# A third score buffer borrowed from the second weights, and identity matmuls between the first tile pairs, in a talking-heads attention and feed-forward kernel

## The chip, the core and the metric

The kernel runs on one core of a Trainium2 chip. The core has five engines that work side by side, each through its own instructions in order: PE (TensorE, matmuls into PSUM), ACT (ScalarE), DVE (VectorE), POOL (GpSimd) and SP (SyncE, which here only issues transfers). ACT and POOL issue transfers too, in line with their other work. Sixteen DMA engines carry the transfers of all queues. The metric is the device time of one execution in microseconds (us), as the median of several runs.

The profile gives each PE matmul its start and a modelled end. It also records the clock that the chip granted to PE: 1.0 is full, 0.5 half. The recorded changes of this clock lie on a grid of 3.41 us.

## The reference

Inputs q, k and v have shape (8, 12, 448, 64): 8 batches, 12 heads, 448 positions, 64 numbers a head. Two 12 x 12 matrices mix heads, w_pre before the softmax and w_post after it.

```python
scores = scale * np.matmul(q, k.transpose(0, 1, 3, 2))
scores = np.einsum('bhij,hg->bgij', scores, w_pre)
attn = softmax(scores)
attn = np.einsum('bhij,hg->bgij', attn, w_post)
x = np.matmul(attn, v)            # to (3584, 768), heads side by side
h = np.maximum(x @ w_in, 0.0)     # w_in (768, 2048)
out = h * h @ w_out               # w_out (2048, 768)
```

(The softmax is written out in the reference; it is named here.)

## The kernel before

**Scores.** For each batch, q and k are loaded, turned on PE (`turn_unit`) and kept as qT and kT. Scores are made a block at a time: a block holds 128 queries of one batch, all 12 heads and 448 keys, as bf16 in a tile S of 128 x 12 x 448. A batch has four blocks (0 to 3). A block is filled by six score pairs (`score_pair`, two heads each): four matmuls of 64 x 64 on 448 columns, one on each quarter of the PE array, and two copies from PSUM to S (L312), one on ACT and one on DVE. S has two buffers, so block 2 takes the buffer of block 0 and block 3 that of block 1.

**Gathers.** Mixing heads needs them on partitions. A tile is 10 queries: `gather` (L329) moves 10 x 12 rows of S to the 120 partitions of a tile G, one DMA a tile. A batch has 45 tiles, the whole kernel 360. G has 12 buffers, and gathers run up to 12 tiles ahead. In the first batch the even tiles' gathers are issued by SP and the odd ones' by ACT; later all by SP. Transfers share eight semaphores, and a gather may have to wait, in its issuing queue, for an earlier one on its semaphore.

**The main loop.** A step `ds` (L461) handles two tiles:

- loads that are due (issued by POOL): k and q of batch 1 come in steps 3 to 8, the eight loads of w2 (the second weights, `load_w2`) in steps 9 to 16, one a step;
- `unmix(ds - 2)`: PE applies w_post to the tiles of two steps before (at_ps, L369), DVE copies the result (at, L374);
- `scores_for(ds)`: some score pairs for later blocks;
- `mix(ds)`: PE applies w_pre to two gathered tiles (m_ps, L338), ACT takes the exponential and its sum (e_sb, L343), DVE the reciprocal (rc, L345), POOL scales and subtracts (d, L347);
- gathers for tiles further on;
- filler: the feed-forward work that is ready (ffn1: h_ps, L234; ffn2: o_ps, L267), spread over the steps by `fill`.

After step 9 the first 16 tiles of batch 0 are done, and step 10 begins with `av_unit` (ot_ps, L185), attention times v for them; the first feed-forward filler comes a step later.

Ahead of the loop stand the turning of batch 0, its blocks 0 and 1, the first ten gathers, and the loads of w1 and v.

**What sets the order.** PE and POOL run in the order in which the program is written (`tc.manual_schedule`). The other engines' order comes from the framework's scheduler. PSUM has eight banks, handed out through one pool (`bank`); whoever takes a bank waits for the engine that last read it.

**How many pairs a step issues** is set in `scores_for`. In batch 0 this line paces them, from the position of the step within a block (`into` of `size`):

```python
want = NPAIR * (blk + 1) + -(-NPAIR * into // size)
```

It gives no pairs in steps 0 and 1 and two in step 2. The scores of batch 0's block 2 are made in steps 2 to 7, those of block 3 from step 8 on.

**The second weights.** w2 is held in four tiles of 128 x 4 x 768 bf16, loaded in halves; its first reader is the ffn2 filler that enters at step 25.

Of the kernel before, what the change touches and what calls it, by code (L numbers as in the profile page):

```python
# [8 lines left out]
BF16 = mybir.dt.bfloat16  # L9
# [5 lines left out]
B, H, S, D = 8, 12, 448, 64  # L15
DMODEL = H * D
DFF = 2048
NPAIR = H // 2
FT = DFF // 128
# [11 lines left out]
PARTS = [[0, 16, 32, NT], [0, 15, 31, NT]]  # L31
LAG = 2
# [10 lines left out]
def kernel(  # L43
# [11 lines left out]
    nc = tc.nc  # L55
    P = nc.NUM_PARTITIONS

    consts = ctx.enter_context(tc.tile_pool(name="consts", bufs=1))
    wts = ctx.enter_context(tc.tile_pool(name="wts", bufs=1))
    stage = ctx.enter_context(tc.tile_pool(name="stage", bufs=1))  # L60
    work = ctx.enter_context(tc.tile_pool(name="work", bufs=1))
# [4 lines left out]
    def bank(name, dtype=F32):  # L66
        return psp.tile([P, 512 if dtype == F32 else 1024], dtype, name=name, tag="ps")
# [11 lines left out]
    ident = consts.tile([P, P], BF16, name="ident")  # L79
# [53 lines left out]
    cgblk = consts.tile([P, NPAIR], F32, name="cgblk")  # L133
    wpost_bf = consts.tile([H, H], BF16, name="wpost_bf")
    w1 = [wts.tile([P, NPAIR, DFF // 4], BF16, name=f"w1_{x}") for x in range(4)]
    w2 = [wts.tile([P, FT // 4, DMODEL], BF16, name=f"w2_{x}") for x in range(4)]

    qTs, kTs, bvecs, xts, h2ts, ats = {}, {}, {}, {}, {}, {}

# [59 lines left out]
    def av_units(b, part):  # L199
        return [(800, lambda cp=cp: av_unit(b, part, cp)) for cp in range(2)]  # L200
# [20 lines left out]

    def load_w2(x):
        n = DFF // 8
        c = x % 2 * 2
        nc.gpsimd.dma_start(out=w2[x // 2][:, c:c + 2, :],
                            in_=moe_w_out[n * x:n * x + n, :].rearrange("(c p) m -> p c m", p=P))

    def ffn1_unit(b, ft, half, c0=0, c1=S):
# [22 lines left out]
    def store_rows(b, mt, osb):  # L251
        t, end = 128 * mt, 128 * mt + ROWS[mt]
        while t < end:
            r, p = divmod(t, PR)
            n = min(end - t, PR - p)
            j = t - 128 * mt
            nc.sync.dma_start(out=out_rows[b, r, p:p + n, :], in_=osb[j:j + n, :])
            t += n

    def ffn2_unit(b, mt, nt, part):  # L260
        if part == 0:
            o_open[(b, mt, nt)] = bank("o_ps")
        ps = o_open[(b, mt, nt)]
        for ft in range(4 * part, 4 * part + 4):
            for n2 in ((nt,) if mt < 3 else (0, 1)):
                dst = ps[:, 0:384] if mt < 3 else ps[64 * n2:64 * n2 + 64, 0:384]
                nc.tensor.matmul(dst, lhsT=h2ts[(b, ft)][:, mt * 128:mt * 128 + ROWS[mt]],  # L267
                                 rhs=w2[ft // 4][:, ft % 4, n2 * 384:(n2 + 1) * 384], start=(ft == 0), stop=(ft == FT - 1))
        if part < 3:
            return  # L270
        if mt < 3:
            if nt == 0:
                osbs[b] = ffnp.tile([P, DMODEL], F32, name="osb", tag="osb", bufs=2)
            nc.vector.tensor_copy(out=osbs[b][:, 384 * nt:384 * nt + 384], in_=ps[:, 0:384])  # L274
            if nt == 1:
                store_rows(b, mt, osbs[b])
        else:
            osb = ffnp.tile([P, 384], F32, name="osb3", tag="osb3", bufs=1)
            nc.vector.tensor_copy(out=osb[:, :], in_=ps[:, 0:384])
            r, p = divmod(128 * mt, PR)  # L280
            for n2 in range(2):
                nc.sync.dma_start(out=out_rows[b, r, p:p + 64, n2 * 384:(n2 + 1) * 384],
                                  in_=osb[64 * n2:64 * n2 + 64, :])
# [13 lines left out]
    Sb, Gs, dsb = {}, {}, {}  # L297

    def score_pair(n):

        b, blk, p = n // (4 * NPAIR), n // NPAIR % 4, n % NPAIR
        if (b, blk) not in Sb:
            Sb[(b, blk)] = work.tile([P, H, S], BF16, name="S", tag="S", bufs=2)
        pss = [bank("s_ps") for _ in range(2)]
        for hh in range(2):
            rs = slice(64 * hh, 64 * hh + 64)
            for z in (0, 64):
                q0 = BLK_START[blk] + z
                nc.tensor.matmul(pss[hh][z:z + 64, 0:S], lhsT=qTs[b][rs, p, q0:q0 + 64], rhs=kTs[b][rs, p, :],  # L309
                                 start=True, stop=True)  # L310
        for hh, copy in enumerate((nc.scalar.copy, nc.vector.tensor_copy)):
            copy(out=Sb[(b, blk)][:, 2 * p + hh, :], in_=pss[hh][:, 0:S])  # L312
# [4 lines left out]
    def needs(s):  # L317
        b, t = s
        return 4 * NPAIR * b + NPAIR * (t // TPB + 1)
# [61 lines left out]
    def at_step(i, unit):  # L381
        timed.setdefault(i, []).append(unit)

    def fill(ns):
# [5 lines left out]
        if not filler:  # L390
            owed[0] = min(owed[0], 0.0)

    steps = [(b, t) for b in range(B) for t in range(NT)]
    with tc.manual_schedule(engines={PE, POOL}):
        for x in range(4):
# [9 lines left out]
        def at_load(i, f, *args):  # L405
            loads.setdefault(i, []).append(lambda: f(*args))
# [6 lines left out]
        for x in range(2, 8):  # L413
            at_load(-1, load_w1, x)
        for x in range(8):
            at_load(18 + 2 * x, load_w2, x)
        for x in range(6):
            at_load(6 + 2 * x, load_qk, 1, x)
            at_load(46 + 2 * x, load_qk, 2, x)
# [12 lines left out]
        def scores_for(ds, most):  # L432
            tile = 2 * ds + AHEAD + 2
            blk = sum(tile >= x for x in starts) - 1
            if blk + 1 >= len(blocks):
                want = NPAIR * len(blocks)
            elif blk in (3, 4):
                want = NPAIR * 4 + 2 * max(0, ds - FIRST_TURN[0])
            else:
                into, size = tile - starts[blk] - 2, starts[blk + 1] - starts[blk] - 2  # L440
                want = NPAIR * (blk + 1) + -(-NPAIR * into // size)
            want = min(want, issued[0] + most, NPAIR * min(blk + 2, len(blocks)))
            k = min(2 * ds + 8, len(steps) - 1)
            want = max(want, needs(steps[k]))
            while issued[0] < want and issued[0] % NPAIR < turned.get(issued[0] // (4 * NPAIR), 0):
                score_pair(issued[0])
                issued[0] += 1

        def gathers_for(ds):
            while gathered[0] < min(2 * ds + AHEAD + 2, len(steps)):  # L450
                if issued[0] < needs(steps[gathered[0]]):
                    break
                gather(gathered[0])
                gathered[0] += 1

        gathers_for(-1)
        for n in range(NPAIR, 2 * NPAIR):
            score_pair(n)
        for f in loads.get(-1, []):
            f()  # L460
        for ds in range(nd + LAG):  # L461
            for i in (2 * ds, 2 * ds + 1):
                for f in loads.get(i, []):
                    f()
            now2 = steps[2 * ds:2 * ds + 2]
            old2 = steps[2 * (ds - LAG):2 * (ds - LAG) + 2] if ds >= LAG else []
            for b, t in now2:
                if t == 0:
                    if b == 0:
                        at_step(ds + 6, (100, cg_unit))  # L470
                    if b + 1 < B:
                        for x, u in enumerate(turn_units(b + 1)):
                            at_step(ds + TURN.get(b, TURN[B])[x], u)
            rest = ((NT + 1) // 2 + LAG + 2 - ds) % (NT / 2) + 1
            if EARLY[2] < ds <= EARLY[2] + 2:
                rest = NT // 2
            elif ds <= EARLY[2]:
                rest = 1 + min(x for x in EARLY if x >= ds) - ds
            share = sum(w for w, _ in filler) / rest if now2 else 1e9
            now = timed.pop(ds, [])  # L480
            for w, f in now:
                f()
            if old2:
                unmix(ds - LAG)
                for b1, t1 in old2:
                    ends = PARTS[b1 % 2]
                    if t1 + 1 in ends:
                        part = ends.index(t1 + 1) - 1
                        for x, u in enumerate(av_units(b1, part)):
                            at_step(ds + (2 + x if b1 else 1), u)  # L490
                        if b1 == 0:
                            c = (IQ * ends[part], min(IQ * ends[part + 1], S))
                            at_step(ds + 1, (0, lambda c=c: filler.extend(ffn1_units(0, *c))))
                    if t1 == NT - 1:
                        if b1 > 0:
                            at_step(ds + 3, (0, lambda b1=b1: filler.extend(ffn1_units(b1))))
                        at_step(ds + (3 if b1 else 1), (0, lambda b1=b1: filler.extend(ffn2_units(b1))))
            scores_for(ds, 2 if ds < NT // 2 or not now and ds % 4 == 0 else 1)
            if now2:
                mix(ds)  # L500
            gathers_for(ds)
            if ds + 1 < nd + LAG:
                fill(share)
        for j in sorted(timed):
# [33 lines left out]
```

The softmax here doesn't subtract the row's maximum and nothing guards it: scores larger than these inputs give would overflow.

## Time and profile before

| | |
|---|---|
| median of 8 runs | 615.39 us (612.52 to 616.74) |
| time of the profiled execution | 615.66 us |
| its span | 613.9 us |
| mean granted clock | 0.964 |
| PE busy | 556.8 us (91%), 11154 matmuls |
| DVE busy | 433.8 us (71%) |
| POOL busy | 396.8 us (65%) |
| ACT busy | 395.0 us (64%) |
| DMA moved | 74.10 MB, mean 121 GB/s |

The span is what the profiler saw from the first instruction to the last; the time of the same execution is 1.8 us longer. Sums are made against these two and then set beside the median.

The page's second part cuts the span into 40 slices of 15.3 us:

```profile
PE   4457888899899999999999899999999999999997
...
DVE  4466999987787778777786768776887788765101
ACT  2456577566688766887578755786678757972320
POOL 7265738557469964897469944798468845892450
```

Each digit is a slice's busy share in tenths. PE is the fullest row from the ninth slice on. The first four slices are the emptiest of PE's row; DVE's row is full from the fifth to the eighth. In the timeline and in the tables of groups, a row names engine, source line, operation, what is written and read, and in square brackets how long the engine stood idle before it and what ended that. Entries such as ACTq or SPq are transfers being issued.

### The profile page before, as it was taken

The numbers are of one execution on the slowest core, as the hardware profiler recorded it, in microseconds if no ns is written. First come the engines' busy times: TensorE is split into PE (matmuls) and PEld (weight loads), VectorE is DVE, ScalarE is ACT, GpSimd is POOL, SyncE is SP. The second block draws the span as 40 slices with busy tenths as digits, with TensorE's granted clock in tenths as the row PEclk, the third lists the DMA queues.
The fourth block names the chain that finished last, engine by engine and source line by source line (L and its number), as shares of the span: only waits on it lengthen the run. The fifth ranks groups of instructions, "written<-read, shape, count | busy, mean of one in ns | idle before, by whom it ended". The sixth has DMA issues, their size and how long they took to land.

```text
span 613.9 us, 26843 instructions
## 1 busy us (share of the span) xinstructions
PE 556.8 (91%) x11154; PEld 313.6 (51%) x11154; DVE 433.8 (71%) x1123; ACT 395.0 (64%) x1196; POOL 396.8 (65%) x579
## 2 busy tenths in 40 slices
PE   4457888899899999999999899999999999999997
PEld 3124566554455456545555456545555455555554
DVE  4466999987787778777786768776887788765101
ACT  2456577566688766887578755786678757972320
POOL 7265738557469964897469944798468845892450
PEclk9756999999899999999999999999999999999999
DMA  9989949859555875488446875478543665431102
GB/s 134 226 169 184 198 93 151 146 89 175 132 126 102 135 147 127 96 141 151 113 109 100 136 144 125 93 122 146 131 103 74 109 146 120 85 65 54 40 15 75
DMA packets 90911, 74.10 MB, mean 121 GB/s; under 512 B 6309, under 2 KB 87717, under 8 KB 90789
## 3 DMA queue, kind: packets, MB, share of 16 engines
q1 hardware_dynamic: 48982, 47.20, 32.9%
q0 software_dynamic: 38816, 22.81, 28.5%
q10 hardware_dynamic: 2990, 2.37, 1.2%
q8 instruction: 87, 1.43, 0.9%
q14 instruction: 36, 0.29, 0.1%
HBM read 45.63 MB, written 11.01 MB: 92 GB/s over the span
## 4 chain that ended last, share of the span: by engine, by line
PE 64%; DVE 10%; POOL 10%; DMA 8%; ACT 4%; issue 3%; ACTq 1%; DVEq 0%; POOLq 0%; SPq 0%
PE o_ps L267 22%; PE h_ps L234 18%; PE at_ps L369 7%; DMA G<-S 6%; PE ot_ps L185 6%; DVE at L374 5%; POOL d L347 5%; PE m_ps L338 5%; POOL h L246 3%; PE tr_ps L162 3%; PE s_ps L309 3%; ACT e_sb L343 2%; DVE S L312 1%; ACT xt L196 1%; DVE h L246 1%
## 5 line engine op out<-in xcount | busy, mean ns | idle before, releaser
L347 POOL TENSOR_SCALAR d<-e_sb,rc 128x448 bf16<-128x448 f32 x360 | 227.3, 643 | 172.5 <-DVE rc L345 170.6
L374 DVE CAST at<-at_ps 112x480 bf16<-112x480 f32 x360 | 219.7, 650 | 44.7 <-PE at_ps L369 42.0
L343 ACT ACTIVATE e_sb<-m_ps 128x448 f32<-128x448 f32 x360 | 195.8, 558 | 21.7 <-POOL d L347 9.6
L234 PE MATMUL h_ps<-xt,w 128*128 128x448 bf16 (+2 forms) x960 | 163.6, 317 | 3.3 <-DVE at L374 2.0
L267 PE MATMUL o_ps<-w,h 128*128 128x384 bf16 (+1 forms) x1024 | 163.9, 330 | 0.6 <-ACT xt L196 0.5
L312 ACT CAST S<-s_ps 128x448 bf16<-128x448 f32 x192 | 100.3, 540 | 85.8 <-PE s_ps L309 60.1
L312 DVE CAST S<-s_ps 128x448 bf16<-128x448 f32 x192 | 115.5, 615 | 12.1 <-DMA G<-S 9.3
L267 PEld LDWEIGHTS <-h 128*128 128x128 bf16 (+1 forms) x1024 | 83.2, 101 | 73.5 <-issue 28.5
L234 PEld LDWEIGHTS <-w 128*128 128x128 bf16 x960 | 79.8, 98 | 79.9 <-issue 31.0
L246 POOL TENSOR_TENSOR h<-hr 128x448 bf16<-128x448 f32 (+2 forms) x124 | 109.1, 888 | 17.1 <-ACT hr L244 17.1
L369 PE MATMUL at_ps<-post,d 60*64 60x60 bf16 x5760 | 86.9, 196 | 15.0 <-POOL d L347 8.3
L369 PEld LDWEIGHTS <-d 60*64 60x64 bf16 x5760 | 64.5, 110 | 59.7 <-issue 23.7
L338 PE MATMUL m_ps<-G,pre 64*64 64x448 bf16 x720 | 78.7, 366 | 16.5 <-DMA G<-S 6.6
L244 ACT ACTIVATE hr<-h_ps 128x448 f32<-128x448 f32 (+2 forms) x136 | 68.8, 512 | 27.9 <-PE h_ps L234 12.1
L345 DVE RECIPROCAL rc<-sm 128x1 f32<-128x1 f32 x360 | 50.3, 156 | 42.2 <-ACT e_sb L343 40.4
L343 ACT ACTIVATION_READ_ACCUMULATOR e_sb<-m_ps 128x1 f32 x360 | 78.2, 217 | 0.0
L196 ACT ACTIVATE xt<-ot_ps,bvec 128x160 bf16<-128x160 f32 (+3 forms) x144 | 44.6, 384 | 50.5 <-PE ot_ps L185 38.8
L309 PE MATMUL s_ps<-kT,qT 64*64 64x448 bf16 x768 | 71.2, 369 | 5.0 <-ACT S L312 4.1
L274 DVE COPY osb<-o_ps 128x384 f32<-128x384 f32 x48 | 26.0, 547 | 40.5 <-PE o_ps L267 40.4
L185 PE MATMUL ot_ps<-at,v 112*64 112x160 bf16 (+4 forms) x1152 | 47.3, 234 | 2.8 <-DVE at L374 2.8
L185 PEld LDWEIGHTS <-v 112*64 112x64 bf16 x1152 | 39.8, 112 | 15.8 <-issue 15.3
L338 PEld LDWEIGHTS <-pre 64*64 64x64 bf16 x720 | 27.6, 108 | 34.7 <-issue 25.8
(39 smaller groups left out, 212.7 us busy)
## 6 DMA issues: line engine op xcount, KB each, us to landing
G<-S SPq DMA_DIRECT2D x330, 105.0 KB
kst<-in_k_dram POOLq DMA_DIRECT2D x24, 224.0 KB, 5.9
qst<-in_q_dram POOLq DMA_DIRECT2D x24, 224.0 KB, 5.8
v<-in_v_dram POOLq DMA_DIRECT2D x24, 224.0 KB, 6.2
w<-in_moe_w_in_dram POOLq DMA_DIRECT2D x8, 384.0 KB, 13.5
w<-in_moe_w_out_dram POOLq DMA_DIRECT2D x8, 384.0 KB, 8.3
out_dram<-osb SPq DMA_DIRECT2D x8, 336.0 KB
G<-S ACTq DMA_DIRECT2D x22, 105.0 KB
```

The lines of the kernel that those rows point to most:

```text
L185: nc.tensor.matmul(ps[64 * hh:64 * hh + 64, TW * y + c0:TW * y + 2 + n], lhsT=vs[b][0:PR, g, r, :], rhs=at[0:PR, r, g, c0:2 + n], start=(y ...
L234: nc.tensor.matmul(ps[:, 0:n], lhsT=w1[ft // 4][:, c2, ft % 4 * 128:ft % 4 * 128 + 128], rhs=xts[b][:, c2, c0:c1], start=(c2 == 0), stop=( ...
L244: nc.scalar.activation(out=hr[:, 0:n], in_=ps[:, 0:n], func=ACT.Relu)
L246: square.tensor_tensor(out=h2ts[(b, ft)][:, c0:c1], in0=hr[:, 0:n], in1=hr[:, 0:n], op=ALU.mult)
L267: nc.tensor.matmul(dst, lhsT=h2ts[(b, ft)][:, mt * 128:mt * 128 + ROWS[mt]], rhs=w2[ft // 4][:, ft % 4, n2 * 384:(n2 + 1) * 384], start=(f ...
L309: nc.tensor.matmul(pss[hh][z:z + 64, 0:S], lhsT=qTs[b][rs, p, q0:q0 + 64], rhs=kTs[b][rs, p, :], start=True, stop=True)
L312: copy(out=Sb[(b, blk)][:, 2 * p + hh, :], in_=pss[hh][:, 0:S])
L338: nc.tensor.matmul(pss[y][64 * x:64 * x + 64, 0:S], lhsT=pre[rows, :], rhs=gs[x][rows, :], start=True, stop=True)
L343: nc.scalar.activation(out=e[:, :], in_=pss[y][:, 0:S], func=ACT.Exp, scale=SCALE, accum_out=sm[:, 0:1])
L347: nc.gpsimd.tensor_scalar(out=d[:, 0:S], in0=e[:, :], scalar1=rc[:, 0:1], scalar2=-1.0 / S, op0=ALU.mult, op1=ALU.add)
L369: nc.tensor.matmul(us[x][z:z + 64, c:c + HR], lhsT=d[rows, PR * r + z:PR * r + z + 64], rhs=post[rows, :], start=True, stop=True)
L374: nc.vector.tensor_copy(out=dst, in_=src)
```

## The change

**Room for a score block.** w2 becomes two tiles of half the weights each. The second half's room is a one-buffer tile that is handed out twice: first as S for block 2 of batch 0, then to the last four loads of w2. Those four loads come at step positions six tiles later (steps 16 to 19 instead of 13 to 16). All other blocks keep the two S buffers.

**Pace of the scores.** In steps 0 to 11, one score pair a step.

**Matmuls on the identity.** `spin(n)` takes two PSUM banks and issues n groups of four matmuls, identity times identity repeated to 448 columns, one on each quarter of the array. Nothing reads the result. `spin(8)` stands ahead of the main loop, `spin(4)` in steps 0 to 9 after the gathers are issued.

```diff
-    w2 = [wts.tile([P, FT // 4, DMODEL], BF16, name=f"w2_{x}") for x in range(4)]
+    half2 = FT // 2 * DMODEL
+    w2 = {0: wts.tile([P, half2], BF16, name="w2_0")}
+
+    def shared_half():
+        return wts.tile([P, half2], BF16, name="w2_1", tag="w2_1", bufs=1)
+
+    def w2_part(x):
+        return w2[x][:, :].rearrange("p (c m) -> p c m", m=DMODEL)
...
-        c = x % 2 * 2
-        nc.gpsimd.dma_start(out=w2[x // 2][:, c:c + 2, :],
+        c = x % 4 * 2
+        if x == 4:
+            w2[1] = shared_half()
+        nc.gpsimd.dma_start(out=w2_part(x // 4)[:, c:c + 2, :],
...
-                                 rhs=w2[ft // 4][:, ft % 4, n2 * 384:(n2 + 1) * 384], start=(ft == 0), stop=(ft == FT - 1))
+                                 rhs=w2_part(ft // 8)[:, ft % 8, n2 * 384:(n2 + 1) * 384], start=(ft == 0), stop=(ft == FT - 1))
...
-            Sb[(b, blk)] = work.tile([P, H, S], BF16, name="S", tag="S", bufs=2)
+            if (b, blk) == (0, 2):
+                Sb[(b, blk)] = shared_half()[:, 0:H * S].rearrange("p (h s) -> p h s", s=S)
+            else:
+                Sb[(b, blk)] = work.tile([P, H, S], BF16, name="S", tag="S", bufs=2)
...
+    def spin(n):
+        pss = [bank("spin_ps") for _ in range(2)]
+        for _ in range(n):
+            for z in (0, 64):
+                rhs = ident[z:z + 64, 0:64].unsqueeze(1).to_broadcast([64, S // 64, 64])
+                for x in (0, 64):
+                    nc.tensor.matmul(pss[z // 64][x:x + 64, 0:S], lhsT=ident[z:z + 64, 0:64], rhs=rhs,
+                                     start=True, stop=True)
...
-            at_load(18 + 2 * x, load_w2, x)
+            at_load(18 + 2 * x + (6 if x > 3 else 0), load_w2, x)
...
+            elif ds < 2 * NPAIR:
+                want = 2 * NPAIR + 1 + ds
...
+        spin(8)
         for f in loads.get(-1, []):
             f()
...
             gathers_for(ds)
+            if ds < PARTS[0][1] // 2 + LAG:
+                spin(4)
             if ds + 1 < nd + LAG:
```

## The prediction

> **What bounds the kernel now.** I read four views in this order. First the clock row of the page's slices, to see where the matrix clock was not granted; then a table of stretches (busy us of PE, PEld, DVE, ACT, POOL in each, then granted clock, share of the DMA engines, GB/s), cut first into the kernel's stages and then into the 3.41 us steps in which the clock changes; then the waits; then the timeline where the waits lie.
>
> ```profile
> PEclk9756999999899999999999999999999999999999
> ...
> 24.90:59.35 34.45, 20.70 (x458) 11.11 (x459) 18.74 (x53) 20.55 (x64) 18.07 (x28) 0.53 1.00 187
> 59.35:68.35 9.00, 8.11 (x228) 6.08 (x231) 8.56 (x27) 6.72 (x23) 8.16 (x13) 1.00 0.98 175
> 68.35:150.00 81.65, 70.06 (x1676) 45.80 (x1660) 75.63 (x204) 53.42 (x173) 53.25 (x84) 0.98 0.78 138
> 150.00:557.00 407.00, 396.20 (x8224) 214.99 (x8223) 307.09 (x771) 295.35 (x899) 286.22 (x412) 0.99 0.61 118
> ```
>
> From 150 us on PE is busy 97% of the time; from 68 to 150 us DVE is, at 93%. Both stages do a fixed amount of work, so what starts them earlier ends the kernel earlier. From 24.9 us (first tile pair mixed, step 0) to 59.35 us (step 11) no engine is busy for more than 60% and the clock is half for nearly all of it: eleven steps take 34.5 us. This is the stretch that the change touches. What holds it:
>
> ```profile
> 35.72 0.97 ACT L312 CAST S<-s_ps 128x448 bf16<-128x448 f32 x2 [5.07 <-DMA G<-S]
> ...
> 36.75 1.11 PE L338 MATMUL m_ps<-G,pre 64*64 64x448 bf16 x4
> ...
> 49.73 0.53 ACT L312 CAST S<-s_ps 128x448 bf16<-128x448 f32 x1 [2.49 <-DMA G<-S]
> ...
> 53.70 3.45 PE L185 MATMUL ot_ps<-at,v 112*64 112x162 bf16 x48 [1.35 <-DVE at L374]
> ```
>
> Twice ACT stands still in front of a score copy until gathers have landed: 5.07 us before block 2's first copy (its buffer is block 0's, still read by the last gathers) and 2.49 us before block 3's (block 1's buffer). Step starts, from the m_ps rows: step 2 at 30.66, 3 at 36.75, 4 at 39.42, 8 at 47.72, 9 at 51.76, 10 at 57.54, 11 at 59.35. Undisturbed steps (4 to 8) take 8.30/4 = 2.08 us; 2 to 3 takes 6.09, 8 to 9 4.04, 9 to 10 5.78. The last holds the attention-times-v matmuls, 3.45 us at half clock; the same 48 take 1.85 us at full clock later (row below).
>
> **Part 1, the room of its own.** Block 2 then waits for nobody, block 3 takes block 0's buffer (all its gathers landed by 35.2 us, by the last of the 120 packets of each on its queue) and step 3 need not wait for ACT. Also one score pair a step is issued from step 0 (before: none in 0 and 1, two in 2 and in 8); a pair costs ACT 0.54 and DVE 0.61, both busy for at most 60% there. Gains: steps 2 to 3 fall from 6.09 to about 2.5 (worked out below), **-3.6**; steps 3 to 9 from 15.01 to 6 x 2.08 = 12.5, **-2.5**.
>
> Its cost is in the weights: four loads of w2 move from steps 13 to 16 to steps 16 to 19. On POOL the first of them waits for all twelve gathers of block 2; behind it stand the d rows (L347) of the next steps, and behind those PE's unmix. The last such gather (tile 35) landed at 65.5 us, step 15 began at 68.35: 2.8 us in hand, and unmix runs two steps later, so I take 0; if that cover went, POOL would be late by the gather's own delay. The loads are still early: step 19 began at 85.34, landing takes 8.3 us by the page's row, the first use is at step 25, 103.58. Four issues of 0.74 us move to a stretch where POOL is 65% busy (68 to 150 us): 0. In exchange 1.5 MB no longer compete with the gathers before step 16.
>
> **Part 2, the matmuls on the identity.** 8 groups of four before step 0, then 4 groups after each of steps 0 to 9: 32 + 160 matmuls of 64 x 64 on 448 columns. The nearest rows are the score matmuls, of the same form on the same four quarters of the array:
>
> ```profile
> 45.02 0.56 PE L309 MATMUL s_ps<-kT,qT 64*64 64x448 bf16 x4
> ...
> 46.99 0.94 PE L309 MATMUL s_ps<-kT,qT 64*64 64x448 bf16 x8
> ...
> 57.35 0.36 PE L309 MATMUL s_ps<-kT,qT 64*64 64x448 bf16 x4
> ...
> 80.29 1.85 PE L185 MATMUL ot_ps<-at,v 112*64 112x160 bf16 x48
> ...
> 82.35 0.55 PE L309 MATMUL s_ps<-kT,qT 64*64 64x448 bf16 x8
> ```
>
> Four more cost 0.94 - 0.56 = 0.38 us at half clock, 0.55 - 0.36 = 0.19 at full. So 4 groups are 1.5 us cold, 0.76 us warm. Against a step of 2.08 us: at full clock unmix 0.44, scores 0.19, mix 0.19 and these 0.76 make 1.6 of 2.08, so they fit. Cold they don't: 0.64 + 0.38 + 0.38 + 1.5 = 2.9.
>
> Does the clock rise? In the stretches below (of one clock step each) I add up the columns that the matmuls stream, four quarters as one, at the prices above.
>
> ```profile
> 19.53:22.95 3.42, 0.11 (x2) 0.00 (x0) 1.28 (x3) 0.00 (x0) 0.43 (x1) 1.00 1.24 216
> ...
> 40.01:43.43 3.42, 2.84 (x78) 1.50 (x78) 3.13 (x10) 2.90 (x10) 3.38 (x6) 0.50 0.94 140
> ...
> 53.67:57.08 3.41, 3.38 (x49) 3.18 (x50) 0.70 (x4) 1.01 (x4) 2.23 (x4) 0.50 0.87 167
> 57.08:60.49 3.41, 2.64 (x91) 1.77 (x90) 2.71 (x7) 3.11 (x10) 0.89 (x2) 1.00 1.05 187
> ```
>
> The array streams 0.00 of the first, then the clock is half; 0.56 of the second, it stays half; 0.95 of the third, it is full; 0.51 of the fourth, it stays full. Over the whole trace it falls after stretches of at most 0.33 and holds from 0.38 up; it rises after 0.77 or more and not after 0.66. With the added work a cold step streams over 0.85, so the first whole stretch after 27.6 us lifts the clock, between 31 and 34.5 us; warm steps stream (0.76 + 0.19 + 0.19 + 0.2)/2.08 = 0.64 and hold it. The 8 groups ahead fill 1.5 of 3.4 us (0.45) in PE's gap before step 0 and cost nothing; but the stretch around step 0 has one mix and one score pair, so it falls again and steps 0 to 2 are cold.
>
> What the clock is worth: the Trainium skill (TensorE: Matmul & The Clock Gate, Terms) prices throttled time at time x (1 - K/N), here 34.1 us x 0.5 = 17 us. The trace says less: in the ten cold stretches the array streams 13.5 us in all, of which full clock saves half, 6.8 us, and most of it lies beside waits. I take only what stands on the path: ot_ps, 3.45 to 1.85, **-1.6**. Undisturbed steps stay at 2.08, because ACT (0.54 + 2 x 0.6 and a gather issue, nearly 2.0) and POOL (2 x 0.63 + 0.73 for a k or q load) need it too.
>
> **The start, where it costs.** PE takes its work in order, and the order of the built program shows what stands ahead: a score pair now precedes step 0's mix and waits for a bank that ACT's late block 1 copies free (25.29 to 27.57, five of them); the first 4 groups wait for the last two of these copies, the second 4 for both exponentials of step 0; and ACT issues gather 11 (0.80) before the new copy and these. So: groups 27.6 to 29.1; pair 13 and step 1's mix to 29.9; ACT 27.1 + 0.8 + 0.54 + 1.2 = 29.7, groups 29.9 to 31.4; unmix 0.64, pair 14 0.38, step 2 at 32.4 instead of 30.66: **+1.7**. Then groups (clock rising within them), unmix and pair: step 3 at about 34.9, against 36.75. Ends for the unknown (when the clock rises): 34.3 to 35.5.
>
> **Sum.** +1.7 - 3.6 - 2.5 - 1.6 = -6.0: step 9 at 47.4, step 10 at 51.6, step 11 at 53.4 instead of 59.35. The gathers allow it: their pairs land every 2.04 us from 24.2 (pair 11 at 49.0 before, needed at 53.4). The DVE and PE stages carry it to the end. The profiled run has 613.9 us of span and 615.66 of time, the median of the runs is 615.39; 615.4 - 6.0 = **609.4 us**.
>
> **Rivals.**
> (a) *The clock doesn't rise, slower.* If added matmuls stay cold, each of the ten steps carries 1.5 us where PE was idle about 0.56 (its wait for POOL's d at 44.17): +0.94 x 10 = 9.4, less 3.6 + 2.5 from the room: +3.3, **618.7**. It decides if the clock stays half for more than six of the ten steps. For it: stretches up to 0.66 did not lift the clock, the same page (Part 4) says that transposes against the identity do not count as busy, and bank waits could leave holes. Against: these are plain matmuls, and the stretch from 12.71 to 16.12, three quarters of it transposes by number, did lift it at 0.77. 13%.
> (b) *Partly.* Steps of 2.4 us instead of 2.08 in 3 to 9, because two of eight PSUM banks are lent out and PE's order ties scores to the step before's exponentials, or because the gathers fall to 2.3 us a pair as they did beside the k and q loads: 6 x 0.32 = 1.9 lost, and 1 more if the clock rises late: -3.1, **612.3**. 17%.
> (c) *Given back later.* If the transfers, not the engines, pace 59 to 83 us (DMA share about 1 there), step 16 starts no earlier: -0 to -1, **614.9**. Against: four of the loads leave exactly this stretch, and DVE is busy there. 10%.
>
> The forecast's own range is 607.5 to 611.5, 60%. The range of 8 in 10 reaches from 606 (clock up already at step 0, steps under 2.0) over (b) to 614.0. A measurement here tells 0.3% (1.85 us) from nothing: faster is the forecast with (b), 0.77; same is (c), 0.10; slower is (a), 0.13.
>
> **What would show it.** ACT's waits for gathers at 35.7 and 49.7 gone (step 2 to 3 near 2.5 us); the clock row half only from about 26 to 33 us; ot_ps 1.85 us in step 10; step 11 near 53.4 us with the same distance from there to the end. Wrong if step 2 starts after 33.5 us, if the clock row stays half to 50 us, or if step 11 gains 6 us and the end does not.

## The result, and the profile after

| | before | after |
|---|---|---|
| median | 615.4 us (612.4 to 617.3, 33 runs) | 606.96 us (603.67 to 612.12, 12 runs) |
| ratio, 95% interval | | 0.987 [0.9848, 0.9893] |
| profiled execution | 615.66 us | 608.57 us |
| its span | 613.9 us | 606.5 us |
| mean granted clock | 0.964 | 0.985 |

The change makes the kernel 8.4 us faster by the medians (615.4 - 606.96) and 7.1 us by the two profiled executions. The forecast was 609.4; 606.96 lies 0.5 us below its own range (607.5 to 611.5) and inside its wider one (606 to 614).

The page's slices of after, 15.2 us each. PE's second and third digits are higher than before, DVE's third, and the clock's second to fourth:

```profile
PE   4697887998999999999999899999999999999997
...
DVE  5496999987987788777786588777887778755101
...
PEclk9898999899999999999999899999999999999999
```

Stretches of after, cut at its own steps 0, 11 and 15 and then by stage (busy us of PE, PEld, DVE, ACT, POOL with counts, then granted clock, share of the DMA engines, GB/s):

```profile
26.25:52.93 26.68, 22.79 (x622) 15.67 (x620) 18.82 (x53) 20.06 (x63) 18.05 (x28) 0.88 1.07 212
52.93:64.01 11.08, 8.85 (x226) 6.68 (x227) 9.73 (x31) 6.54 (x23) 9.29 (x14) 0.87 0.95 183
64.01:142.00 77.99, 67.18 (x1645) 44.80 (x1634) 72.88 (x198) 52.12 (x169) 51.52 (x81) 0.98 0.81 141
142.00:550.00 408.00, 397.31 (x8252) 215.93 (x8250) 308.27 (x776) 296.21 (x904) 287.08 (x413) 1.00 0.61 119
```

Steps 0 to 11 take 26.68 us where they took 34.45, with the same work on DVE, ACT and POOL (18.82, 20.06 and 18.05 us against 18.74, 20.55 and 18.07): what went is waiting. DVE still fills 93% of the third stretch and PE 97% of the last, so both carry the gain on. The DMA engines are now full in the first stretch (1.07).

PE's timeline of after, from the first step to the eleventh, with one row of ACT's:

```profile
25.81 1.02 PE L322 MATMUL s_ps<-kT,qT 64*64 64x448 bf16 x4 [4.17 <-ACT S L325]
26.25 1.01 PE L351 MATMUL m_ps<-G,pre 64*64 64x448 bf16 x4
...
31.93 0.47 PE L351 MATMUL m_ps<-G,pre 64*64 64x448 bf16 x4
...
33.73 0.53 ACT L325 CAST w<-s_ps 128x448 bf16<-128x448 f32 x1
...
33.81 0.38 PE L351 MATMUL m_ps<-G,pre 64*64 64x448 bf16 x4
...
45.74 0.95 PE L412 MATMUL spin_ps<-ident 64*64 64x448 bf16 x16
47.06 1.87 PE L193 MATMUL ot_ps<-at,v 112*64 112x162 bf16 x48 [0.37 <-DVE at L387]
48.86 0.31 PE L382 MATMUL at_ps<-post,d 60*64 60x60 bf16 x13
51.26 0.35 PE L382 MATMUL at_ps<-post,d 60*64 60x60 bf16 x19 [2.09 <-issue]
51.42 0.38 PE L322 MATMUL s_ps<-kT,qT 64*64 64x448 bf16 x4
51.61 0.38 PE L351 MATMUL m_ps<-G,pre 64*64 64x448 bf16 x4
```

The copy into block 2 (it writes w, the room of the weights) has no bracket any more: ACT waits for no gather there. The score pair that now stands ahead of step 0 waits 4.17 us for ACT. The attention-times-v matmuls take 1.87 us. New is the last bracket: PE stands still for 2.09 us in the middle of a group, and nothing in the trace releases it ("issue").

What sets the pace between steps 3 and 9 now? POOL's timeline of after goes on like this from 33.88 to past 45 us:

```profile
37.08 0.74 POOL L73 DMA_DIRECT2D qst<-in_q_dram  x1
37.86 1.25 POOL L360 TENSOR_SCALAR d<-e_sb,rc 128x448 bf16<-128x448 f32 x2
39.06 0.73 POOL L73 DMA_DIRECT2D kst<-in_k_dram  x1
39.83 1.25 POOL L360 TENSOR_SCALAR d<-e_sb,rc 128x448 bf16<-128x448 f32 x2
```

From 35.08 to 46.40 us no row has a bracket: two d rows and the issue of one k or q load follow each other without a gap, 1.97 us a step (39.83 - 37.86). In this profile POOL is the limit there.

Step starts from the m_ps rows (us), with the experiments that follow:

| step | before | after | e1_room | e2_spin | e3_full | e8_double | e9_full28 |
|---|---|---|---|---|---|---|---|
| 2 | 30.66 | 31.93 | 30.02 | 31.01 | 30.25 | 32.56 | 30.27 |
| 3 | 36.75 | 33.81 | 32.62 | 37.56 | 31.87 | 34.75 | 32.28 |
| 9 | 51.76 | 45.55 | 46.36 | 52.23 | 46.47 | 50.01 | 45.03 |
| 10 | 57.54 | 51.61 | 51.90 | 56.87 | 50.10 | 54.29 | 49.03 |
| 11 | 59.35 | 52.93 | 53.37 | 58.69 | 51.92 | 56.10 | 50.86 |
| 20 | 88.90 | 82.06 | 82.16 | 88.76 | 80.72 | 84.89 | 79.66 |
| 45 | 163.91 | 156.23 | 158.29 | 164.43 | 155.97 | 159.77 | 155.31 |
| 179 | 557.74 | 550.38 | 550.04 | 555.90 | 549.30 | 551.53 | 547.23 |

### The profile page after: what moved, and what is told of

The parts are those of the page before. It is cut to its first block, busy times and chain, and to the rows that moved or that the text cites. A ratio compares the mean times of both kernels' runs of the same rounds, so it can differ in the third digit from the quotient of the medians.

```text
span 606.5 us, 27220 instructions
## 1 busy us (share of the span) xinstructions
PE 559.9 (92%) x11346; PEld 319.8 (53%) x11346; DVE 433.2 (71%) x1123; ACT 394.6 (65%) x1196; POOL 397.1 (65%) x579
## 4 chain that ended last, share of the span: by engine, by line
PE 63%; POOL 12%; DVE 10%; DMA 6%; ACT 4%; issue 3%; ACTq 0%; DVEq 0%; POOLq 0%; SPq 0%
PE o_ps L277 21%; PE h_ps L244 18%; PE at_ps L382 7%; POOL d L360 6%; PE ot_ps L193 6%; DVE at L387 5%; DMA G<-S 5%; PE m_ps L351 4%; POOL h L256 4%; PE s_ps L322 3%; PE tr_ps L170 3%; DVE S L325 2%; ACT e_sb L356 2%; ACT xt L204 1%; POOL qst L73 1%
## 5 line engine op out<-in xcount | busy, mean ns | idle before, releaser
L325 ACT CAST S<-s_ps 128x448 bf16<-128x448 f32 x186 | 97.0, 540 | 79.4 <-PE s_ps L322 60.3
L256 POOL TENSOR_TENSOR h<-hr 128x448 bf16<-128x448 f32 (+2 forms) x124 | 109.1, 887 | 17.1 <-ACT hr L254 17.1
L325 DVE CAST S<-s_ps 128x448 bf16<-128x448 f32 x186 | 111.9, 615 | 5.8 <-DMA G<-S 3.9
L204 ACT ACTIVATE xt<-ot_ps,bvec 128x160 bf16<-128x160 f32 (+3 forms) x144 | 44.5, 385 | 49.3 <-PE ot_ps L193 39.5
L193 PE MATMUL ot_ps<-at,v 112*64 112x160 bf16 (+4 forms) x1152 | 45.8, 229 | 1.8 <-DVE at L387 1.8
L193 PEld LDWEIGHTS <-v 112*64 112x64 bf16 x1152 | 38.4, 109 | 14.6 <-issue 14.1
```

The lines of the kernel that those rows point to most:

```text
L193: nc.tensor.matmul(ps[64 * hh:64 * hh + 64, TW * y + c0:TW * y + 2 + n], lhsT=vs[b][0:PR, g, r, :], rhs=at[0:PR, r, g, c0:2 + n], start=(y ...
L256: square.tensor_tensor(out=h2ts[(b, ft)][:, c0:c1], in0=hr[:, 0:n], in1=hr[:, 0:n], op=ALU.mult)
```

## The experiments

The intervals of the ratios are some ±0.3%, about 1.8 us; a single profile shows where time lies, not a difference of 1 us between kernels. (e3_full and e11_full8 are one kernel, and their profiles have step 2 at 30.25 and 31.81 us.)

**The two parts, each alone.** e1_room is the changed kernel without its identity matmuls; e2_spin is the old kernel with them.

```diff
 e1_room, against the changed kernel
-        spin(8)
...
-            if ds < PARTS[0][1] // 2 + LAG:
-                spin(4)
 e2_spin, against the old kernel
+        spin(8)
...
+            if ds < PARTS[0][1] // 2 + LAG:
+                spin(4)
```

> The changed kernel without the matmuls on the identity (room for block 2, one score pair a step, moved w2 loads stay). Theory (the sum of the prediction): the two waits for gathers go, -6.1, the start costs under +1.4 because no identity matmuls stand ahead of the unmix; PE stays at half clock to step 10, so the attention-times-v matmuls stay at 3.45 us. About 610 us, step 3 near 34.5, step 11 near 54.5. Rival (the clock carries the gain: at half clock one pair a step is on the path): under half of the gain, 612 to 614 us, steps 4 to 8 at 2.3 us or more.

> The kernel before with only the matmuls on the identity added. Theory: both waits for gathers stay (about 5 and 2.5 us), the clock rises between them but falls again in the long one, the attention-times-v matmuls are at full clock; -1 to -2, about 614 us. Rival 1 (clock carries the gain): 610 us or less. Rival 2 (the added matmuls cost on PE's path): 616 to 619 us.

e1_room: 608.61 us, ratio 0.9889 [0.9863, 0.9915]. e2_spin: 613.88 us, 0.9973 [0.9956, 0.999]. So 1.11% and 0.27%, together 1.38%; the whole change gave 1.3%. The room (with the pace and the moved loads) is most of the gain. The matmuls on the identity add little: on the old kernel just clear of nothing, and on top of the room not told from nothing, since the interval of e1_room takes in the 0.987 of the changed kernel.

In e2_spin the clock rises (mean 0.76 from 24.9 us to step 11, against 0.53), but ACT's timeline still has the two stops in front of block 2's and block 3's first copies:

```profile
34.84 0.53 ACT L312 CAST S<-s_ps 128x448 bf16<-128x448 f32 x1 [4.33 <-DMA G<-S]
...
50.16 0.53 ACT L312 CAST S<-s_ps 128x448 bf16<-128x448 f32 x1 [2.54 <-DMA G<-S]
```

A faster PE only comes to the same wait. In e1_room these two stops are gone and the clock stays half; its stretch from step 4 to step 9, and its step 10 from PE's timeline:

```profile
34.60:46.36 11.76, 8.54 (x207) 3.81 (x202) 9.68 (x28) 7.93 (x25) 9.73 (x16) 0.50 1.04 196
```

```profile
47.71 3.45 PE L193 MATMUL ot_ps<-at,v 112*64 112x162 bf16 x48 [0.77 <-ACT e_sb L356]
```

Five steps take 11.76 us, 2.35 each, at half clock with PE busy 73%; ot_ps costs its cold 3.45 us. It still reaches step 11 only 0.44 us after the changed kernel, and its profiled execution (608.23 us) is no slower than that kernel's (608.57). Step 3 came at 32.62, earlier than the 34.5 expected. The rival's sign, steps of 2.3 us or more, is there, its time is not; and by the trace it is not the half clock that lengthens the steps. POOL's timeline of e1_room, then a piece of the chain of work that ended last in the window from 33 to 47 us (start, us, what):

```profile
36.68 1.25 POOL L360 TENSOR_SCALAR d<-e_sb,rc 128x448 bf16<-128x448 f32 x2
37.89 0.73 POOL L73 DMA_DIRECT2D kst<-in_k_dram  x1
40.15 0.63 POOL L360 TENSOR_SCALAR d<-e_sb,rc 128x448 bf16<-128x448 f32 x1 [1.53 <-DVE rc L358]
...
42.49 1.25 POOL L360 TENSOR_SCALAR d<-e_sb,rc 128x448 bf16<-128x448 f32 x2
43.69 0.73 POOL L73 DMA_DIRECT2D kst<-in_k_dram  x1
44.46 1.25 POOL L360 TENSOR_SCALAR d<-e_sb,rc 128x448 bf16<-128x448 f32 x2
```

```profile
28.13 9.77 DMA G<-S
37.90 0.02 issue
37.92 0.83 ACTq L342
```

At half clock too, an undisturbed step takes POOL 1.97 us (42.49 to 44.46). What is lost lies in the gap before 40.15: by this chain, a gather that took 9.77 us holds up ACT's issue of a later gather at 37.92, ACT's score copy and exponentials come behind it, and POOL has nothing to work on. The same window of e3_full, e9_full28, e10_full0 and e11_full8, with the clock mostly full, has a gather of 7.9 to 8.8 us in its chain as well; that of after has none. In these six kernels step 9 comes between 45.03 and 46.86 us, though step 3 lies anywhere from 31.87 to 33.95. That the gathers set this limit is read from the chains and not tested by itself.

**The pace of the scores.** e5_oldpace is e1_room without the two lines that issue one pair a step.

```diff
-            elif ds < 2 * NPAIR:
-                want = 2 * NPAIR + 1 + ds
```

> The changed kernel with the room and the moved loads alone: no matmuls on the identity, and score pairs in the old pace (none in steps 0 and 1). Room and new pace without these matmuls took 608.6 us. Theory: the room carries that gain, both waits for gathers need it; without the earlier pairs the start loses nothing (step 2 at 30.7 or before) and block 2 is finished a step later, which its gathers have in hand: 608 to 610 us. Rival (the pace carries part): 611 to 613 us, because tiles 24 and 25 are gathered a step later.

610.57 us, 0.991 [0.9885, 0.9935], a little above the range expected; step 2 at 30.59, as expected, and step 10 at 52.65 us against 51.90 in e1_room. The intervals of the two overlap widely: the pace may be worth the 0.2% between them, or nothing. The room with the moved loads makes 0.9% by itself, most of the 1.1% of e1_room.

**The moved weights.** e6_w2early has the four loads back in their old steps, into the shared room.

```diff
-            at_load(18 + 2 * x + (6 if x > 3 else 0), load_w2, x)
+            at_load(18 + 2 * x, load_w2, x)
```

> The changed kernel with the last four w2 loads in their old steps, 13 to 16. The prediction priced their move at 0 and named the gathers of block 2 as what the first of them waits for. Theory: at step 13 (57.8 us) tile 35's gather (landed at 61.9 us in the changed kernel's trace) is 4 us away; POOL waits for it with the d rows of the next steps behind, so steps 14 to 16 start 2 to 4 us late: 609 to 611 us. Rival (two steps of slack hide it): 607 us.

612.18 us, 0.9944 [0.9916, 0.9972]: a little above the range expected, and more than half of the gain is gone. All engines' timeline at the first load into the room:

```profile
61.50 0.74 POOL L235 DMA_DIRECT2D w<-in_moe_w_out_dram  x1 [3.49 <-DMA G<-w]
62.28 1.25 POOL L360 TENSOR_SCALAR d<-e_sb,rc 128x448 bf16<-128x448 f32 x2
...
62.98 0.32 PE L382 MATMUL at_ps<-post,d 60*64 60x60 bf16 x16 [2.56 <-POOL d L360]
```

POOL waits 3.49 us to issue the load, until the last gather has read block 2 (G<-w). The d rows of two tiles stand behind it in POOL's order, PE's unmix behind those: PE loses 2.56 us. Moving the loads is thus part of the change's gain and not a price of it.

**Twice the matmuls.** e8_double issues `spin(8)` after each of steps 0 to 9.

> The changed kernel with 8 groups in each of steps 0 to 9 instead of 4. Theory: 4 groups (0.76 us) fit beside the other engines' step of 1.96 us, 8 groups (1.5 us) don't: PE needs 0.82 + 1.5 = 2.35 us a step, and 104 to 144 rows more a step are fetched, so ten steps cost +4 or more: 611 to 613 us. Rival (PE's work is free up to there, as gathers at 2.04 us a pair pace the steps): 607 to 608 us.

613.89 us, 0.9966 [0.9936, 0.9997], just above the range expected; step 11 comes 3.2 us later than in the changed kernel. (The profile is of the fastest of ten executions, 609.72 us, so it shows the cost at its smallest.) The stretch from 34 to 44 us of e8_double, then the same of after:

```profile
34.00:44.00 10.00, 10.00 (x342) 7.21 (x337) 8.68 (x26) 6.73 (x22) 8.30 (x13) 1.00 0.99 193
```

```profile
34.00:44.00 10.00, 9.10 (x291) 6.24 (x284) 9.94 (x28) 8.13 (x26) 9.83 (x16) 1.00 1.03 204
```

With eight groups PE is never idle and DVE and POOL get less done (8.68 and 8.30 us instead of 9.94 and 9.83). With four, DVE and POOL are the full ones: PE's row counts the groups, but they lie in time that was free. (The 104 to 144 rows "more" of the expectation are a step's whole count: 730 records in the six steps from 36.94 to 50.01 us, of which the added groups are 32 a step.)

**The stall without a releaser.** Count PE's matmuls and weight loads, each one record. The stalls on "issue" of after of 0.5 us or more come when 1471 (2.09 us), 1982 (1.48), 3517 (0.83) and 3773 (1.01) records have begun: 511, 1535 and 256 apart, multiples of 256 but for one record. Other kernels stall at counts that fit the same multiples within two records, at other times: e4_long and e7_no8 at 1215, e6_w2early and e8_double at 1471 (49.87 and 48.21 us), e2_spin at 1982, e3_full at 1725. The queue that the page calls q8, "instruction", carries packets of 16 384 bytes, 64 bytes for each of 256 records. Four groups of four cost 32 records a step. e3_full does each group as one matmul on the whole array, with the same streaming time and 8 records a step. It also takes one PSUM bank for them instead of two.

```diff
-        pss = [bank("spin_ps") for _ in range(2)]
+        ps = bank("spin_ps")
+        rhs = ident[:, 0:64].unsqueeze(1).to_broadcast([P, S // 64, 64])
...
-            for z in (0, 64):
-                rhs = ident[z:z + 64, 0:64].unsqueeze(1).to_broadcast([64, S // 64, 64])
-                for x in (0, 64):
-                    nc.tensor.matmul(pss[z // 64][x:x + 64, 0:S], lhsT=ident[z:z + 64, 0:64], rhs=rhs,
-                                     start=True, stop=True)
+            nc.tensor.matmul(ps[:, 0:S], lhsT=ident[:, :], rhs=rhs, start=True, stop=True)
```

> The changed kernel with each group of four 64 x 64 identity matmuls replaced by one of 128 x 128: the same columns streamed, two PE instructions a group instead of eight. Theory (PE's stall of 2.09 us at 49.2 us is the fetch of its next 256 instructions, 16 KB, which the added instructions use up faster than a busy DMA brings them): the stall goes or shrinks, clock row as before it, -1 to -2 against the changed kernel, 605 us. Rival (the stall is something else, or the clock counts quarter matmuls differently): 607 us as the changed kernel or slower.

607.55 us, 0.9874 [0.9851, 0.9896]: no different in time from the changed kernel, and not the 605 expected. The stall near 49 us is gone (one of 1.27 us comes at 62.31) and step 9 to 10 takes 3.63 us instead of 6.06. But ACT waits once for a gather (first line), PE has less to do, and the clock is half for a stretch right after (the others):

```profile
36.66 0.53 ACT L325 CAST w<-s_ps 128x448 bf16<-128x448 f32 x1 [2.10 <-DMA G<-S]
```

```profile
35.49:38.90 3.41, 2.35 (x46) 0.99 (x44) 1.99 (x6) 1.80 (x6) 2.42 (x5) 1.00 0.99 197
38.90:42.32 3.42, 3.42 (x48) 1.29 (x46) 3.23 (x10) 3.00 (x10) 2.99 (x5) 0.50 1.07 216
```

This is not the kernel's habit: the second profile of it, e11_full8, has the full clock from 31.68 to 147.73 us.

**The groups ahead of the loop.** The prediction gave the eight groups ahead neither cost nor gain. e7_no8 leaves them out; e4_long makes them 28, to hold the clock up from 15 us on.

> The changed kernel without the 8 groups of identity matmuls ahead of the loop; the 4 groups of steps 0 to 9 stay. Theory: the clock falls before step 0 with them or without, since PE has nothing to do for 3 to 4 us after them; they are worth nothing: 607 us, clock half until about 32 us. Rival (they keep the clock for step 0 in some runs): 608 to 609 us.

> The changed kernel with 28 groups of identity matmuls ahead of the loop instead of 8: at 0.19 us each they fill PE's idle gap up to about 24.8 us, where nothing else can run. Theory: the clock is still full at step 0, so steps 0 to 2 run at full clock; step 2 near 30.6 instead of 31.9, -1 to -1.5 against the changed kernel. Rival 1 (ACT, not PE, sets steps 0 to 2): no change. Rival 2 (the fetch of 160 more instructions beside the loads): slower by 1 us or more.

e7_no8: 610.29 us, 0.9903 [0.988, 0.9927]. e4_long: 608.87 us, 0.9888 [0.9847, 0.993]. Fewer and more are both a little worse by the median, with intervals that overlap that of the changed kernel; neither expectation (607 us; 1 to 1.5 us faster) is met. Of the 3.3 us of e7_no8 its profile shows 1.1 at step 11 and 3.2 more from step 41 to 44, which the groups ahead do not touch; what makes it slower stays open. In e4_long the clock is full without a break from 15.6 to 152 us and step 2 comes at 30.70, 1.2 us earlier, but PE also stalls more before step 12: 0.73 us at 41.62 and twice again (PE's timeline):

```profile
48.09 0.38 PE L351 MATMUL m_ps<-G,pre 64*64 64x448 bf16 x3 [1.25 <-issue]
...
54.53 0.28 PE L382 MATMUL at_ps<-post,d 60*64 60x60 bf16 x11 [1.89 <-issue]
```

Since the stalls move with the count of records, both kernels mix two effects. The whole-array form keeps them apart: e10_full0 (no group ahead), e11_full8 (8, e3_full again) and e9_full28 (28) ran together on one chip. The edit of e9_full28 against e11_full8:

```diff
-        spin(8)
+        spin(28)
```

> As e3_full, without any group ahead of the loop. Theory of the prediction (these groups cost and gain nothing): ratio as that of the same kernel with 8 groups within 0.0015, step 2 near 30.2 us. Rival (they shorten the cold time, as the clock is half from one grid step earlier without them): clock half from about 21 to 31 us, step 3 later by 0.5 to 1.5 us, ratio higher by 0.002 or more.

> The kernel of e3_full again, on the chip of the two others of this call, so that 0, 8 and 28 groups ahead stand beside each other: ratio 0.987 as before (0.985 to 0.990). If the number of groups ahead matters, the three ratios fall in the order 0, 8, 28; if not, they agree within 0.002.

> As e3_full (each group one matmul of 128 x 128 on 448 columns), but 28 groups ahead of the loop instead of 8. Theory (an early full clock is worth something once the groups cost PE few rows to fetch): the clock stays full from about 15 us to past 60 us, step 2 starts near 30 us, and PE waits on 'issue' for at most 0.7 us per fetch boundary up to step 11; step 11 between 51 and 52.5 us, time 605 to 607 us, ratio 0.983 to 0.986. Rival (the gathers, one pair every 2.04 us, set the steps whatever the clock): steps 3 to 9 are no faster than with 8 groups, ACT or PE waits for gathers instead, time 607 to 609 us, ratio 0.987 to 0.989.

608.19, 607.29 and 607.82 us; ratios 0.9885 [0.986, 0.991], 0.988 [0.9847, 0.9912] and 0.9878 [0.9847, 0.991]. The three agree within 0.0007: by the times, the groups ahead are worth nothing that can be told, as the prediction had it; e9_full28 misses the 605 to 607 us expected of it. The profiles are less plain. In e10_full0 the clock is half from 21.08 to 31.32 us, as its rival had it, without the loss in time. e9_full28 has the full clock from 15.9 to 104.6 us, no stall on "issue" of 0.5 us or more before step 11, and step 11 at 50.86, two us ahead of the changed kernel. Its tenth step in PE's timeline, with nothing standing between ot_ps and the step's mix:

```profile
46.77 1.87 PE L193 MATMUL ot_ps<-at,v 112*64 112x162 bf16 x48 [0.51 <-DVE at L387]
48.57 0.44 PE L382 MATMUL at_ps<-post,d 60*64 60x60 bf16 x32
48.84 0.36 PE L322 MATMUL s_ps<-kT,qT 64*64 64x448 bf16 x4
49.03 0.36 PE L351 MATMUL m_ps<-G,pre 64*64 64x448 bf16 x4
```

The lead of 2.4 us at step 20 has shrunk to 0.9 at step 45 and is 3.2 at step 179. From step 41 to 44, where PE waits once for an ACT copy (1.80 us in after, 2.11 in e9_full28), after took 10.43 us and e9_full28 11.92, with the clock at half from 149 us on. Such a stretch of half clock, starting between 147 and 158 us, stands in twelve of the thirteen profiles; only that of after is without it. The median of e9_full28 does not show the lead: its six runs lie between 605.4 and 609.6 us, and the two at 605.44 have mean clocks of 0.994 and 1.000. None of the variants is measurably faster than the changed kernel.

## Why the prediction was right, step by step

**Room, steps 2 to 3 and 3 to 9: right in kind, under-sized.** Both of ACT's stops went, as e1_room shows without any help from the clock. Step 2 to 3 took 1.88 us (33.81 - 31.93), not about 2.5. Steps 3 to 9 took 11.74, or 1.96 each, not 12.5. The clause "undisturbed steps stay at 2.08" had the mechanism right, and its term for POOL, 2 x 0.63 + 0.73 = 1.99, was nearer than the 2.08 that was used: POOL's rows repeat every 1.97 us in after, and in e1_room at half clock as well. The same six steps took 13.74 in e1_room and 12.75 in e9_full28; the rows shown above put e1_room's extra time on a late gather, and not on the clock. That after met no such gather is read from one profile, so part of its 11.74 may be luck.

**Start: right, slightly over-sized.** +1.7 was forecast at step 2, +1.3 measured. Of the two reasons given, the score pair and the cold groups ahead in PE's order, the groups are the one that counts: e1_room has the pair and not the groups, and step 2 at 30.02, 1.9 us earlier than after and 0.6 earlier than before.

**Clock: right.** The clock row of the changed kernel, in stretches of one clock step (columns as above):

```profile
21.75:25.17 3.42, 0.00 (x0) 0.00 (x0) 0.00 (x0) 0.00 (x0) 0.00 (x0) 1.00 1.19 246
...
28.58:31.99 3.41, 3.41 (x68) 2.42 (x64) 1.23 (x6) 2.00 (x7) 2.50 (x4) 0.50 1.10 230
31.99:35.41 3.42, 3.17 (x116) 2.56 (x109) 3.41 (x8) 3.21 (x10) 1.53 (x3) 1.00 0.74 170
...
49.06:52.47 3.41, 1.27 (x76) 0.97 (x63) 0.90 (x3) 1.73 (x6) 0.62 (x1) 1.00 1.15 217
52.47:55.89 3.42, 3.42 (x56) 2.19 (x53) 3.18 (x11) 2.61 (x10) 2.29 (x4) 0.50 1.01 156
```

It is half from 25.17, after the empty stretch, and up from 31.99, in the window given (31 to 34.5 us); steps 0 to 2 were cold, as forecast. The second dip, from 52.47 to 55.89, was not forecast (see step 9 to 10). ot_ps was priced at -1.6 and measured 1.58 shorter (3.45 to 1.87). The matmuls by themselves, in e2_spin, gave 0.27% of 615.4, 1.7 us [0.6, 2.7]. The rule weighed against this, throttled time x (1 - K/N) from the Trainium skill (TensorE: Matmul & The Clock Gate, Terms), can be tried on the two kernels that differ by these matmuls alone: up to step 13 e1_room has 30.7 us of half clock (21.85 to 52.57), the changed kernel 10.2 (6.8 and 3.4). The rule makes 10.2 us of the 20.5 between them; the medians differ by 1.65 (608.61 - 606.96), within the intervals. The old kernel without and with them says the same: up to step 11 before has 34.1 us of half clock (22.95 to 57.08) and e2_spin 17.1 (24.21 to 31.04, 34.45 to 41.28, 51.52 to 54.94); the rule makes 8.5 us of the difference, and 1.7 came. Part of the rest is the price of the matmuls (the start and the stall below); for much of the throttled time PE was not what the others waited for, as POOL's 1.97 us a step at half clock shows.

**What was not foreseen: step 9 to 10.** The working gave it 4.2 us (47.4 to 51.6); it took 6.06. The 2.09 us on "issue" ate the whole gain of ot_ps, and by emptying the stretch from 49.06 on (1.27 of 3.41 us busy) cost another 3.4 us of full clock. e3_full and e9_full28, where no such stall lies, took 3.63 and 4.00 us. That step 10 began at 51.61, as forecast, is two errors that cancel: 1.85 us too early at step 9, 1.9 too long after it. The prediction weighed the added matmuls by PE's time and by bank waits, and not by the records that PE has to fetch.

**Weights: right at 0.** All eight loads of after are issued without a wait, the moved ones at 67.87, 71.15, 75.95 and 79.44 us. The case named beside it, POOL late "by the gather's own delay", is what e6_w2early shows with 3.49 us.

**The end: carried.** -6.4 us at step 11, -6.8 at step 20, -7.4 at step 179. Rival (c), given back later, is out. Rival (a), the cold clock, is out by the clock row. Rival (b), steps of 2.4 us, did not come: they took 1.96. In e1_room, without the matmuls on the identity, they took 2.35 from step 4 on, and that kernel kept most of the gain.

**The sum.** -6.0 was forecast, -7.1 came in the profiled pair: 0.4 of the difference was there at step 11, and the rest came later, above all from step 41 to 44 (10.43 us against 11.57 before), which no step of the prediction touched. There before has the stretch of half clock (156.07 to 159.48) that twelve profiles have and after has not, so this 1.1 us is more likely luck of the one profile than the change. The medians stand 1.3 us further apart than the profiled pair; where that lies, no single profile can tell: the profiled execution of after (608.57 us) is slower than eight of its twelve other runs.

## What to carry to other kernels

When a stage has no busy engine, find the wait that ends last and give it room; a buffer whose real owner comes later is such room, provided that the owner's load is issued after the last reader and not in front of other work in its queue. Matmuls issued only to keep the clock up can pay a little where they fit the step's free time (0.27% on the old kernel here) and cost where they don't (e8_double). Count their instructions as well as their time: in the profiles fewer and larger ones took a stall away, though the medians did not show it. The gain of a granted clock is what stands on the path in the cold time, and not the cold time.

## What the hardware showed unexpectedly

- In after PE stalled for 0.8 to 2.1 us at four counts of its records that lie multiples of 256 apart, in stretches with a DMA share of 0.81 to 1.32. In before one weight load stood 1.03 us on "issue" at 71.75 us, after 1725 records (the profile puts the matmul behind it down to DVE). In after, PE's records went past the boundary before the longest stall at 44.5 us; a packet of the instruction queue began at 48.8 us, and PE went on at 51.26. That the full engines delay the packet is read from the traces and not tested by itself.
- In these traces the clock follows how full the array was in the last 3.41 us (shares added up as in the prediction): from 20 us to the last matmuls of after it fell after 0.00, 0.26, 0.30 and 0.32 and held from 0.44 up; at half it stayed so after 0.60 and rose after 0.80 or more. In e3_full it fell after 0.39, where the trace of before held at 0.38: the edge is not one sharp number.
- A full clock early is worth little by itself: between the medians of e1_room (mean clock 0.968 in its profile) and the changed kernel (0.985) lie 1.6 us, within the intervals, and the 2 us that e9_full28 wins by step 11 with 0.994 did not show in its median.
- Over the thirteen executions of the changed kernel the mean granted clock goes with the time: 0.982 in the slowest (612.12 us), 0.995 in the fastest (603.67 us). Which of the two drives the other, no run here shows.
